# Top-k attention with two feed-forward networks on one core: low parts of late expert weights and relu outputs move from GpSimd to VectorE

## Chip, core and metric

The kernel runs on one core of a Trainium2 chip. The metric is the time of one execution on the device in microseconds (us), as the median of several runs. The engines are named as in the profile: PE is TensorE (PEld its weight loads), DVE is VectorE, ACT is ScalarE, POOL is GpSimd, SP is SyncE, which here only issues DMAs.

## What is computed

Attention with 8 heads over two sequences of 576 positions keeps, per row, only the 32 largest scores. Its output (1152 tokens of 512 values) goes through four gated experts and then through a network with three first matrices whose outputs are joined by a maximum. The matrices of that last network are handed over as 64-bit floats.

```python
scores = q @ k.T / sqrt(64); kth = 32nd largest of each row
attn = softmax(where(scores >= kth, scores, -1e9)); x = attn @ v        # -> (1152, 512)
p = probs / probs.sum(-1)
for e in range(4):                                                      # w1: 512 x 1024, w2: 1024 x 512
    out += p[:, e] * (relu(x @ w1[e]) @ w2[e])
h = maximum(maximum(out @ m1, out @ m2), out @ m3)                      # 512 x 768 each
result = h @ mo
```

## The kernel before

**Three products for one.** A matmul in float32 is replaced by three matmuls in a faster type (`product`, lines 677 to 683). Each operand is split in a high part, a copy in that type made by ScalarE, and a low part, the operand less its high part. TensorE then adds high x low, high x high and low x high (L681 to L683). So every weight and every activation needs a high part from ScalarE and a low part from VectorE or GpSimd before TensorE can go on.

**Tiles and stages.** The tokens are nine tiles of 128. The experts' work goes in stages of one to three tiles, as attention delivers them: stage 0 is tile 0, stages 1 to 6 are pairs of neighbours, stage 7 is tiles 6, 7 and 8, stage 8 is tiles 7 and 8. Each stage applies two of the four experts (`HALVES`), even stages units 0 to 3 and odd ones 4 to 7, a unit being half an expert, 512 hidden columns in two weights for the first layer (keys "a") and two for the second ("b"). Each key is a block of 128 x 1024 values. Attention is over when stage 7 begins. After stage 8 comes the last network in three groups of three tiles, with keys "c" for its first layer and "d" for its second. At its border the sums of the experts are turned on TensorE and split, the low part by L908.

**One weight.** `w_split_to` (257 to 282) walks through the list of keys in the order in which TensorE uses them, four keys ahead of the use (`weight`, `W_AHEAD`). For each it takes a raw buffer that SP's queue has loaded (`w_load_to`, L213; five raw buffers), lets ScalarE make the high part (L272) and then VectorE or GpSimd the low part (L278), into one of five buffers each. `LATE` is 7, and `late` (L274) counts keys from the first "a" key of stage 7. Before that key GpSimd makes all low parts, in two halves of 512 columns. From it on, odd keys go to VectorE in one instruction of 1024 columns and even keys to GpSimd. From stage 7 to the end of the experts there are 34 such keys, two "a" and two "b" by turns; then the "c" and "d" keys follow.

**One relu output.** `half1` makes the first layer of one key. Ordinarily ScalarE writes the relu of the PSUM result as high part (L823), and VectorE takes the relu of the PSUM result again and subtracts the high part (L825). Every fourth time (`ON_POOL_H`) ScalarE writes the relu in full to SBUF (L816), copies it as high part (L817), and GpSimd subtracts (L818). Three tiles need two PSUM banks and so two pieces in L823 and L825. `half2` and `layer2` are the second layer; `gated` (L742, L744) adds its output, times the gate, to the tile's sum.

**Conversions.** The last network's weights come as 64-bit floats. `to_float32` turns them into 32-bit ones in 48 pieces, most of them beside stages 7 and 8: two ScalarE steps (L239, L240), three VectorE steps (L242, L244, L246), one GpSimd step (L249), then a load for a later piece on SP's queue (L223) and a store to memory on ScalarE's queue (L254), each emitted some steps after the one before.

**What sets the order.** Each engine runs its instructions in the order in which the program emits them, and so does each DMA queue. The main loop (992 to 1015) emits a step of attention or conversions, then products until a planner's TensorE time (`pe`) has reached a goal that grows with its VectorE time (`dve`). After attention, each step adds a fixed pause of 0.8 and what was booked for conversions and evacuations. `later` delays the evacuation of a PSUM result by one or more products.

Of the kernel before, what the change touches and what calls it, by code (L numbers as in the profile page):

```python
# [24 lines left out]
ON_POOL_H = 4  # L25
# [5 lines left out]
LATE = 7  # L31
# [29 lines left out]
def kernel(  # L61
# [14 lines left out]
    nc = tc.nc  # L76
# [54 lines left out]
    def dve(n):  # L131
        clock["dve"] += 0.07 + n / 960.0

    def pe(n):
        clock["pe"] += n / 2400.0

    def bank(name):
        return pg.tile([P, 512], F32, tag="g", name=name)
# [62 lines left out]
    def whole(key):  # L201
        return key[1] in "ab" and key[0] in WHOLE

    def w_load_to(n):
        while w_pos["load"] < min(n, len(order)):
            key, src = order[w_pos["load"]]
            if key[1] in "cd" and narrowed[0] < WIDE * (narrow_at[key[2:]] + 1):
                return
            if whole(key):
                w_pos["load"] += 1  # L210
                continue
            raw = wp.tile([P, 1024], F32, tag="raw", bufs=5, name="raw")
            nc.sync.dma_start(out=raw, in_=src)  # L213
            w_raw[key] = raw
            w_pos["load"] += 1
# [41 lines left out]
    def w_split_to(n):  # L257
        while w_pos["split"] < min(n, len(order)):
            w_load_to(w_pos["split"] + 1)
            if w_pos["load"] == w_pos["split"]:  # L260
                return
            key, src = order[w_pos["split"]]
            if whole(key):
                w_hl[key] = wp.tile([P, 1024], F32, tag=("hi", "lo")[key[3]], name="whole")
                nc.sync.dma_start(out=w_hl[key], in_=src)
                w_pos["split"] += 1
                w_load_to(w_pos["split"] + 3)
                continue
            raw = w_raw.pop(key)
            hi = wp.tile([P, 1024], F32R, tag="hi", name="whi")  # L270
            lo = wp.tile([P, 1024], F32R, tag="lo", name="wlo")
            nc.scalar.activation(out=hi, in_=raw, func=AF.Copy)  # L272

            late = w_pos["split"] - w_index[LATE, "a", HALVES[LATE][0], 0]  # L274
            on = nc.vector if late >= 0 and late % 2 else nc.gpsimd

            for x in (slice(0, 512), slice(512, 1024)) if on is nc.gpsimd else (slice(0, 1024),):
                on.tensor_tensor(out=lo[:, x], in0=raw[:, x], in1=hi[:, x].bitcast(F32), op=ALU.subtract)  # L278
            f = 512 if key[1] in "bd" else 256
            w_hl[key] = (hi.rearrange("p (a f) -> p a f", f=f), lo.rearrange("p (a f) -> p a f", f=f))  # L280
            w_pos["split"] += 1
            w_load_to(w_pos["split"] + 3)

    def weight(key, oldest=None):

        w_split_to(w_index[oldest or key] + W_AHEAD + 2 * whole(key))
        return w_hl[key]
# [90 lines left out]
    def xs_of(tiles):  # L378

        at_ = [place(t) for t in tiles]  # L380
        step = max(1, at_[-1] - at_[0]) // max(1, len(at_) - 1)
        assert at_ == list(range(at_[0], at_[-1] + 1, step))
        return [[x[:, a].rearrange("p (s n) -> p s n", n=P)[:, at_[0]:at_[-1] + 1:step] for a in range(KT)] for x in xring]
# [279 lines left out]
    def tick():  # L663
        for x in list(lag):
            x.pop(0)()
            if not x:
                lag.remove(x)
# [5 lines left out]
    def later(*stages):  # L673
        tick()
        lag.append(list(stages))
# [20 lines left out]
    def layer1(wt, xs, N, ps=None):  # L696

        if ps is not None:
            for f in range(2):
                product(spread(ps[:, f * N:(f + 1) * N], xs[0][KT - 1]), [w[:, KT - 1, f * P:(f + 1) * P] for w in wt], [x[KT - 1] for x in xs], False, f == 1)  # L700
            yield [(slice(0, 2 * N), ps[:, 0:2 * N])]
            return
        groups = []
        for f in range(2):
            if not f or 2 * N > 512:
                ps = bank("ps1")
                groups.append((slice(f * N, 2 * N if 2 * N <= 512 else (f + 1) * N), ps[:, 0:min(2 * N, 512) if 2 * N <= 512 else N]))
            to = ps[:, f * N:(f + 1) * N] if 2 * N <= 512 else ps[:, 0:N]
            for a in range(KT):
                product(spread(to, xs[0][a]), [w[:, a, f * P:(f + 1) * P] for w in wt], [x[a] for x in xs], a == 0, a == KT - 1)  # L710
            yield groups if f else None

    def hidden(N):
        if 2 * N <= 512:
            ht = hp_.tile([P, 2, 512], F32R, tag="h", bufs=4, name="h")
            return ht[:, 0, 0:2 * N], ht[:, 1, 0:2 * N]

        assert len(x_ready) == len(pairs) and 2 * N <= 2 * WIDTH
        hh = kv.tile([P, 2, S], F32R, tag="kT", bufs=5, name="hh")
        hl = hp_.tile([P, 2, 512], F32R, tag="h", bufs=4, name="hl")  # L720
        return [x.rearrange("p a n -> p (a n)")[:, 0:2 * N] for x in (hh, hl)]
# [25 lines left out]
    def first_alone():  # L747
# [26 lines left out]
        for e, h in hs.items():  # L774
            ps = po.tile([P, DM], F32, tag="o", name="ps2")
            for y in range(2):
                for u in range(2):
                    w = w_alone["b", 2 * e + y, u]
                    for f in range(2):
                        pe(4 * DM)  # L780
                        nc.tensor.matmul(ps, lhsT=h[:, y, (2 * u + f) * P:(2 * u + f + 1) * P], rhs=w[f],
                                         start=y == u == f == 0, stop=y == u == f == 1)
                        yield True
                    if u:
                        w_split_to(2 * e + y + 1)
                    if e and not y and not u:
                        tick()
            later(gated(ps, 0, e, not e, False))

    def experts():  # L790
        begin = {}

        def half1(c, i, u):
            tiles = STAGES[c]
            N = len(tiles) * P
            if c in WHOLE:
                ps = bank("ps1")
                w = weight((c, "a", i, u)).rearrange("p (a f) -> p a f", f=256)
                for f in range(2):
                    for a in range(KT):  # L800
                        pe(4 * P)
                        nc.tensor.matmul(ps[:, f * P:(f + 1) * P], lhsT=w[:, a, f * P:(f + 1) * P], rhs=xfull[:, a, :], start=f == a == 0, stop=f == 1 and a == KT - 1)
                    yield True
                h = hp_.tile([P, 2, 512], F32, tag="h", bufs=4, name="hfull")[:, 0, 0:2 * P]
                later(lambda: [nc.scalar.activation(out=h, in_=ps[:, 0:2 * P], func=AF.Relu), made.add(("h", c, i, u))])
                yield h
                return
            for groups in layer1(weight((c, "a", i, u)), xs_of(tiles), N, begin.pop((c, i, u), None)):
                if groups is None:
                    tick()  # L810
                    yield True
            hh, hl = hidden(N)
            count = made_h[0] = made_h[0] + 1
            if ON_POOL_H and not count % ON_POOL_H:
                raw = ms.tile([P, 2 * WIDTH], F32, tag="tm", bufs=2, name="raw")
                later(lambda: [nc.scalar.activation(out=raw[:, g], in_=ps, func=AF.Relu) for g, ps in groups],  # L816
                      lambda: [nc.scalar.activation(out=hh[:, 0:2 * N], in_=raw[:, 0:2 * N], func=AF.Copy),  # L817
                               nc.gpsimd.tensor_tensor(out=hl[:, 0:2 * N], in0=raw[:, 0:2 * N], in1=hh[:, 0:2 * N].bitcast(F32), op=ALU.subtract),  # L818
                               made.add(("h", c, i, u))])
                yield hh, hl  # L820
                return
            dve(2 * N)
            later(lambda: [nc.scalar.activation(out=hh[:, g], in_=ps, func=AF.Relu) for g, ps in groups],  # L823
                  *[lambda: None] * H_LAG,
                  lambda: [nc.vector.scalar_tensor_tensor(out=hl[:, g], in0=ps, scalar=0.0, in1=hh[:, g].bitcast(F32),  # L825
                                                          op0=ALU.max, op1=ALU.subtract) for g, ps in groups]
                  + [made.add(("h", c, i, u))])
            yield hh, hl
# [252 lines left out]
```

## Time and profile before

| | before |
|---|---|
| median of three runs | 765.25 us (765.12 to 765.64) |
| the profiled execution | 765.73 us |
| its span (first to last instruction) | 763.9 us |
| busy: PE, PEld | 729.3, 644.0 us |
| busy: DVE, ACT, POOL | 625.9, 508.2, 503.3 us |
| read from memory, written | 120.60, 8.65 MB |

The span is what the profile covers; 1.8 us of the execution lie around it. Stage 7's first matmul starts at 475.5 us of the span and the last network's first one at 606.3 us. A busy engine may also be an engine that waits inside an instruction. Matmuls are pipelined, so the distance between the starts of two matmuls, and not the duration of one, tells TensorE's pace.

### The profile page before, as it was taken

How to read it: one execution, taken by the hardware profiler on the slowest of the kernel's cores; microseconds unless marked ns; L12 is line 12 of the kernel's file. 1: busy time of each engine (PE TensorE's matmuls, PEld its weight loads, DVE VectorE, ACT ScalarE, POOL GpSimd, SP SyncE). 2: the span in 40 equal slices, each digit the busy share in tenths (PEclk: the TensorE clock that was granted, in tenths of full speed). 3: DMA queues.
4: the chain of work that ended last, by engine and by line, in shares of the span. 5: the costliest groups of instructions: out<-in, count | busy, mean ns of one | idle time of the engine just before them, and what ended most of it. 6: DMA issues, size and time to landing. Idle time of an engine off the chain costs nothing. (4 is left out here: it accounts for less than half of the span.)

```text
span 763.9 us, 13775 instructions
## 1 busy us (share of the span) xinstructions
PE 729.3 (95%) x4758; PEld 644.0 (84%) x4758; DVE 625.9 (82%) x1161; ACT 508.2 (67%) x1137; POOL 503.3 (66%) x433
## 2 busy tenths in 40 slices
PE   6899999999999999999999979999999899999998
PEld 3576789888989999888899868998797699999996
DVE  6999989989999899999999979999999844233341
ACT  4668889899896888787788674765656533433431
POOL 2514788599979778788688759867869742442520
PEclk9999999999999999999999999999999999999999
DMA  7693564545637364464445457887878652453501
GB/s 219 183 275 133 160 193 136 149 152 174 183 110 214 97 189 126 135 190 124 146 122 163 137 187 218 274 266 239 291 229 290 209 168 85 134 183 97 193 2 42
DMA packets 56486, 130.16 MB, mean 170 GB/s; under 512 B 9760, under 2 KB 23328, under 8 KB 56416
## 3 DMA queue, kind: packets, MB, share of 16 engines
q1 hardware_dynamic: 48064, 120.69, 50.8%
q10 hardware_dynamic: 8352, 8.59, 3.2%
q8 instruction: 37, 0.61, 0.3%
q14 instruction: 33, 0.27, 0.1%
HBM read 120.60 MB, written 8.65 MB: 169 GB/s over the span
## 5 line engine op out<-in xcount | busy, mean ns | idle before, releaser
L278 POOL TENSOR_TENSOR wlo<-raw,whi 128x512 fp32r<-128x512 f32 x258 | 341.1, 1351 | 116.6 <-ACT whi L272 112.5
L272 ACT ACTIVATE whi<-raw 128x1024 fp32r<-128x1024 f32 x164 | 169.5, 1056 | 47.2 <-POOL narrow L249 19.1
L681 PE MATMUL ps<-xl,whi 128*128 128x256 f32 (+1 forms) x584 | 173.5, 297 | 0.4 <-POOL xl L556 0.4
L682 PE MATMUL ps<-xh,whi 128*128 128x256 f32 (+1 forms) x584 | 170.7, 292 | 0.0
L683 PE MATMUL ps<-xh,wlo 128*128 128x256 f32 (+1 forms) x584 | 170.7, 292 | 0.0
L444 DVE MAX8 m<-work 128x8 f32<-128x576 f32 x216 | 155.0, 743 | 0.1
L681 PEld LDWEIGHTS ps<-xl,whi 128*128 128x128 f32 x584 | 110.7, 190 | 1.5 <-POOL xl L556 0.6
L682 PEld LDWEIGHTS ps<-xh,whi 128*128 128x128 f32 x584 | 109.7, 188 | 0.8 <-issue 0.2
L683 PEld LDWEIGHTS ps<-xh,wlo 128*128 128x128 f32 x584 | 109.6, 188 | 0.0
L446 DVE MATCH_REPLACE8 work<-m,work 128x576 f32<-128x576 f32 x144 | 106.5, 740 | 0.0
L278 DVE TENSOR_TENSOR wlo<-raw,whi 128x1024 fp32r<-128x1024 f32 x35 | 55.5, 1586 | 50.5 <-ACT whi L272 38.2
L681 PE MATMUL ps<-wlo,h 128*128 128x512 f32 x224 | 92.9, 415 | 4.0 <-POOL wlo L278 2.2
L683 PE MATMUL ps<-whi,h 128*128 128x512 f32 x224 | 89.7, 400 | 5.4 <-POOL h L818 5.4
L682 PE MATMUL ps<-whi,h 128*128 128x512 f32 x224 | 89.2, 398 | 0.0
L249 POOL TENSOR_TENSOR narrow<-narrow,raw 128x256 int32<-128x256 int32 x48 | 50.4, 1050 | 32.8 <-DVE narrow L246 10.7
L431 ACT ACTIVATE s<-pss 128x288 f32<-128x288 f32 x144 | 51.4, 400 | 11.4 <-PE pss L419 11.1
L444 DVE MAX8 m<-s 128x8 f32<-128x576 f32 x72 | 53.8, 747 | 4.9 <-ACT s L431 4.9
L683 PEld LDWEIGHTS ps<-whi,h 128*128 128x128 f32 x224 | 42.9, 192 | 17.1 <-POOL h L818 7.5
L681 PEld LDWEIGHTS ps<-wlo,h 128*128 128x128 f32 x224 | 43.6, 195 | 14.9 <-POOL wlo L278 5.6
L446 DVE MATCH_REPLACE8 work<-m,s 128x576 f32<-128x576 f32 x72 | 53.3, 740 | 0.0
L681 PE MATMUL ps<-x2l,whi 128*128 128x384 f32 x144 | 48.8, 339 | 1.3 <-DVE x2l L908 1.3
L948 DVE TENSOR_TENSOR tm<-ps,tm 128x384 f32<-128x384 f32 x36 | 19.9, 555 | 35.2 <-PE ps L683 33.3
(113 smaller groups left out, 1551.9 us busy)
## 6 DMA issues: line engine op xcount, KB each, us to landing
raw<-in_w_dram SPq DMA_DIRECT2D x128, 512.0 KB, 4.1
raw<-narrow SPq DMA_DIRECT2D x36, 512.0 KB, 4.1
raw<-in_m_dram SPq DMA_DIRECT2D x36, 256.0 KB, 4.0
whole<-in_w_dram SPq DMA_DIRECT2D x14, 512.0 KB, 5.7
narrow<-narrow ACTq DMA_DIRECT2D x48, 128.0 KB, 4.1
kraw<-in_k_dram SPq DMA_DIRECT2D x16, 288.0 KB, 4.5
qraw<-in_q_dram SPq DMA_DIRECT2D x48, 64.0 KB, 3.8
raw<-in_mo_dram SPq DMA_DIRECT2D x12, 256.0 KB, 4.7
```

The costliest lines, as they stand in the source:

```text
L249: nc.gpsimd.tensor_tensor(out=out.bitcast(I32), in0=out.bitcast(I32), in1=last, op=ALU.add)
L272: nc.scalar.activation(out=hi, in_=raw, func=AF.Copy)
L278: on.tensor_tensor(out=lo[:, x], in0=raw[:, x], in1=hi[:, x].bitcast(F32), op=ALU.subtract)
L431: nc.scalar.activation(out=s[:, h, :], in_=halves[h][:, 0:SH], func=AF.Copy)
L444: nc.vector.max(m[:, 8 * r:8 * r + 8], src)
L446: nc.vector.match_replace(out=self.w[j], in_to_replace=m[:, 8 * r:8 * r + 8], in_values=src, imm_value=NEG)
L681: nc.tensor.matmul(ps, lhsT=lh, rhs=rl, start=first, stop=False)
L682: nc.tensor.matmul(ps, lhsT=lh, rhs=rh, start=False, stop=False)
L683: nc.tensor.matmul(ps, lhsT=ll, rhs=rh, start=False, stop=last)
L948: nc.vector.tensor_tensor(out=tm[:, g], in0=ps, in1=tm[:, g], op=ALU.max)
```

## The change

The low parts of the "a" and "b" keys from the first one of stage 7 on all go to VectorE. The "c" and "d" keys still alternate. From stage 7 on every relu output is made the ordinary way (L823, L825).

```diff
             late = w_pos["split"] - w_index[LATE, "a", HALVES[LATE][0], 0]
-            on = nc.vector if late >= 0 and late % 2 else nc.gpsimd
+            on = nc.vector if late >= 0 and (late % 2 or key[1] in "ab") else nc.gpsimd
...
             count = made_h[0] = made_h[0] + 1
-            if ON_POOL_H and not count % ON_POOL_H:
+            if ON_POOL_H and not count % ON_POOL_H and c < LATE:
                 raw = ms.tile([P, 2 * WIDTH], F32, tag="tm", bufs=2, name="raw")
```

## Rows read from the trace of the kernel before

**Rows 1.** Windows: busy us (x count) of PE, PEld, DVE, ACT, POOL; clock; DMA

```profile
596.00:599.50 3.50, 1.18 (x5) 0.33 (x3) 3.36 (x6) 2.96 (x9) 2.13 (x3) 1.00 0.80 253
599.50:603.30 3.80, 3.80 (x10) 3.00 (x11) 2.69 (x5) 3.39 (x6) 3.52 (x3) 0.55 0.01 4
...
474.00:605.00 131.00, 124.39 (x668) 108.26 (x666) 127.22 (x164) 79.73 (x153) 102.19 (x81) 0.99 0.79 256
606.30:764.00 157.70, 153.95 (x834) 146.16 (x834) 55.40 (x71) 54.95 (x77) 55.14 (x38) 1.00 0.35 118
```

**Rows 2.** TensorE's waits in 474 to 606.5 us: us in total, times, longest

```profile
PE ps L683 <- POOL hl L818: 2.3, 2, 1.8
PE ps L683 <- POOL h L818: 2.1, 2, 1.2
PE ps L681 <- ACT h L817: 1.4, 1, 1.4
PE ps L681 <- DVE x2l L908: 1.3, 1, 1.3
PE ps L681 <- POOL wlo L278: 0.5, 1, 0.5
PE ps L681 <- DVE wlo L278: 0.2, 1, 0.2
```

**Rows 3.** Line 818, 474 to 605 us: ns min/median/max, first and last start

```profile
L818 POOL TENSOR_TENSOR h<-raw,h x3: 1323/1461/1476, 484.2 to 598.1; 128x512 fp32r<-128x512 f32 x3
```

**Rows 4.** Single lines, 474 to 605 us: ns min/median/max, first and last start

```profile
L246 DVE SCALAR_TENSOR_TENSOR narrow<-raw,narrow x40: 424/426/1487, 473.0 to 604.7; 128x256 uint32<-128x256 uint32 x40
...
L278 DVE TENSOR_TENSOR wlo<-raw,whi x18: 1211/1424/2322, 474.4 to 601.5; 128x1024 fp32r<-128x1024 f32 x18
...
L825 DVE SCALAR_TENSOR_TENSOR hl<-ps,hh x12: 540/543/550, 488.8 to 536.1; 128x384 fp32r<-128x384 f32 x12
L825 DVE SCALAR_TENSOR_TENSOR h<-ps,h x6: 677/680/685, 551.7 to 592.4; 128x512 fp32r<-128x512 f32 x6
...
L244 DVE TENSOR_SCALAR narrow<-raw x39: 293/727/1821, 477.6 to 604.4; 128x256 uint32<-128x256 uint32 x39
...
L242 DVE SCALAR_TENSOR_TENSOR raw<-narrow,raw x39: 408/593/1509, 476.6 to 602.8; 128x256 f32<-128x256 f32 x39
...
L249 POOL TENSOR_TENSOR narrow<-narrow,raw x40: 735/814/1736, 475.5 to 599.8; 128x256 int32<-128x256 int32 x40
```

**Rows 5.** Timeline of TensorE: start us, us, engine, line [idle before and releaser]

```profile
470.33 0.40 PE L681 MATMUL ps<-wlo,h 128*128 128x512 f32 x1
470.57 0.39 PE L682 MATMUL ps<-whi,h 128*128 128x512 f32 x1
...
550.24 0.50 PE L683 MATMUL ps<-whi,hl 128*128 128x512 f32 x1 [1.76 <-POOL hl L818]
```

**Rows 6.** Timeline of GpSimd and VectorE side by side, 466 to 471 us

```profile
466.47 5.47 POOL L278 TENSOR_TENSOR wlo<-raw,whi 128x512 fp32r<-128x512 f32 x4
...
469.39 1.40 DVE L246 SCALAR_TENSOR_TENSOR narrow<-raw,narrow 128x256 uint32<-128x256 uint32 x1
```

**Rows 7.** GpSimd's groups, 474 to 605 us: busy us, mean ns, idle before

```profile
L278 POOL TENSOR_TENSOR wlo<-raw,whi 128x512 fp32r<-128x512 f32 x36 | 52.4, 1478 | 1.0 <-ACT whi L272 0.6
...
L818 POOL TENSOR_TENSOR h<-raw,h 128x512 fp32r<-128x512 f32 x3 | 4.3, 1420 | 0.0
L818 POOL TENSOR_TENSOR hl<-raw,hh 128x768 fp32r<-128x768 f32 x2 | 4.0, 2013 | 0.0
```

**Rows 8.** VectorE's groups, 474 to 605 us: busy us, mean ns, idle before

```profile
L246 DVE SCALAR_TENSOR_TENSOR narrow<-raw,narrow 128x256 uint32<-128x256 uint32 x40 | 31.9, 797 | 1.4
L278 DVE TENSOR_TENSOR wlo<-raw,whi 128x1024 fp32r<-128x1024 f32 x18 | 29.7, 1651 | 1.1 <-POOL narrow L249 1.1
L244 DVE TENSOR_SCALAR narrow<-raw 128x256 uint32<-128x256 uint32 x39 | 28.3, 725 | 1.3
L242 DVE SCALAR_TENSOR_TENSOR raw<-narrow,raw 128x256 f32<-128x256 f32 x39 | 27.7, 709 | 0.0
```

## The prediction

> **What bounds the kernel now.** I read the stretches of the span first, then TensorE's waits, then VectorE's and GpSimd's groups and the durations of single lines. The changed lines act from about 472 us (the first weight of stage 7) to about 605 us (the last weight of the experts). In 474 to 605 us VectorE is busy 127.2 of 131 us and GpSimd 102.2; TensorE is busy too, 124.4, but that is the engine with the work that can't be moved [rows 1]. After 606 us TensorE is busy 154.0 of 157.7 us and VectorE a third of the time [rows 1], so time won before 606 us is kept.
>
> What TensorE loses in the stretch is the second thing to see. It waits 2.3 and 2.1 us for the low parts of relu outputs that GpSimd makes (L818), 1.4 us for ScalarE's copy in front of one of them (L817), 0.5 and 0.2 us for low parts of weights, and 1.3 us for the low part of the turned x2 at the border to the last network [rows 2]. GpSimd makes five such relu parts in this stretch [rows 7], the first of them, at 484 us, still for stage 6 [rows 3]. VectorE makes 12 by L825 (six of stage 7 in two pieces, six of stage 8 in one) [rows 4], and none has a line among TensorE's waits [rows 2].
>
> The third is the clock. In 596.0 to 599.5 us TensorE was busy only 1.18 us, because of two of those waits; in the next 3.8 us its granted clock was 0.55, mostly the 1.2 GHz level, and it issued 10 matmuls [rows 1]. At the full clock such 512-column matmuls start 0.23 us apart [rows 5].
>
> The fourth is why VectorE is full. Its operations with both inputs in SBUF take 0.42 us (L246) or 1.21 us (L278) at the least, but up to 1.49 and 2.32 us [rows 4]. The long ones lie beside GpSimd: four L278 halves run from 466.47 for 5.47 us, and an L246 that begins at 469.39 takes 1.40 us [rows 6]. Operations that read PSUM (L825) keep one duration, 0.54 and 0.68 us, to 10 ns [rows 4]. So GpSimd and VectorE wait for one another, one instruction at a time.
>
> **The change part by part.** Weight keys come in fours (a, a, b, b), 34 of them from the first of stage 7 on; odd ones are on VectorE already, so 17 move.
>
> GpSimd loses 34 halves at 1.478 us, 50.3 us, and four relu parts, 2 x 1.42 + 2 x 2.01 = 6.9 us [rows 7]. It goes from 102.2 to about 45 us in this stretch. By itself that ends nothing; it counts by what waited behind it.
>
> VectorE gains 17 x 1.211 = 20.6 us of weight parts, and for the relu parts 4 x 0.543 + 2 x 0.680 = 3.5 us (two of stage 7 in two pieces, two of stage 8 in one): 24.1 us [rows 4].
>
> VectorE loses its waits for GpSimd. L246, L278, L244 and L242 took 31.9 + 29.7 + 28.3 + 27.7 = 117.6 us [rows 8]. At their least durations they would take 40 x 0.424 + 18 x 1.211 + 39 x 0.293 + 39 x 0.408 = 66.1 us [rows 4]. The excess is 51.5 us. What stays is the last step of the conversion on GpSimd (L249), 40 times. The trace has no stretch with L249 alone beside the new mix, so I bound it: nothing if it falls beside PSUM reads, and its whole least duration each time, 40 x 0.735 = 29.4 us [rows 4]. I take 0.43 us each, the median of L244 less its least, since that median comes from pairs with L249: 17.2 us. VectorE would then be busy 127.2 - 51.5 + 24.1 + 17.2 = 117.0 us, between 99.8 and 129.2. Now it takes 127, so the added work fits only because the waits go. The Trainium skill (SBUF — State Buffer, section Who interferes with whom) has the meeting of the two engines as a lock on a shared port that is held for a whole instruction while the other blocks. The trace agrees as far as rows 6 go; taken at its hardest, with every L249 starting just ahead of a VectorE operation, the rule gives the upper end, 129.2, and my 117.0 takes the shorter waits that the median of L244 shows.
>
> TensorE's side gives the sum. The waits on L818 go, 4.4 us, and the 1.4 us on L817, because the relu part is then made like the other 12: one ScalarE step and one VectorE step instead of two and a GpSimd step. After each of those five waits the first matmul takes 0.50 us instead of 0.39 [rows 5], so 0.5 us more. Without the waits at 596 to 599.5 us I expect no clock drop behind them: 3.8 - 10 x 0.23 = 1.5 us. The 0.7 us on low parts of weights I leave as they are: a late VectorE takes GpSimd's place. The 1.3 us at the border stays as well; the low part of x2 stands in VectorE's queue behind conversions and weight parts that do not move.
>
> New waits: each moved weight part waits on VectorE for ScalarE's high part, and behind it in that queue stand conversions, the relu parts and the sums into the accumulators, which TensorE and ScalarE need. In this stretch VectorE idles so far only 1.1 us, before one L278, and that for GpSimd [rows 8]. The bounds are nothing, and all that is won; I take 1.0 us, nearest to what the 18 weight parts already there cost.
>
> Edits at nothing: four ScalarE copies go (ScalarE is busy 79.7 of 131 us [rows 1]). One instruction of 1024 columns takes 1.21 us where two halves took 2.96, so no low part comes later for that. A raw weight buffer is now freed by VectorE; SP's queue, where the next loads stand, already waits mostly for GpSimd's L249, which comes sooner. L254's store on ScalarE's queue waits for the same step. The planner counts 2.9 us more VectorE time (four sets of 0.87 or 0.60), so some one conversion is issued later against the products: about 1.1 us of VectorE work moves behind 605 us, where VectorE is idle for most of the time. Without that cover it would cost the 1.1 us.
>
> The sum: 4.4 + 1.4 + 0.5 + 1.5 - 1.0 = 6.8 us. The profiled execution took 765.73 us (span 763.9 and 1.8 around it), 0.48 above the median of 765.25. So 758.9 for a like execution, and **758.5 us** as a median.
>
> **The rivals.**
> *All waits go.* Weight parts and the border too, nothing new: 4.4 + 1.4 + 0.5 + 1.5 + 0.7 + 1.3 = 9.8, 755.4 us. For it: VectorE at 117 us is below what TensorE needs, about 123. Against: the border hangs on a queue that hardly changes.
>
> *Half comes back.* A weight part waits at the head of VectorE's queue for its high part and holds a relu part: half of the 6.8 is lost, 761.9 us. For it: ScalarE itself is held by stores that wait for conversions. Against: VectorE has not waited for ScalarE in this stretch [rows 8].
>
> *Same.* VectorE's relu parts come as late as GpSimd's did, because VectorE runs behind: 765 us. Against: none of the 12 was waited for.
>
> *Slower.* VectorE becomes the bound in stages 7 and 8. It decides from the point where its waits for L249 exceed 27.4 us (99.8 of work without them, 3.8 idle as now, 131 of stretch). If all forty block for a whole L249, 29.4 us, the stretch is 133.0 us and the time 767.3 us. For it: VectorE is at 97% and gets more work. Against: the 51.5 us of waits lie mostly beside the GpSimd halves that go. The Trainium skill (Perfetto Trace Analysis, section Optimizing Scalar/DVE Operations) advises the opposite of this change, to offload a saturated VectorE, though it adds that between these two engines it might not help, for the shared port. By the first half alone, with none of the waits gone, the 24.1 us would be added: 789.4 us. No row bears that out so far.
>
> That the change does something else than it says has little room: the keys before stage 7 and those of the last network keep their engine, and I have counted them so.
>
> **How the numbers follow.** Forecast, 756.5 to 760.5 us: 0.57. All waits go: 0.12. Half comes back: 0.13. Same: 0.07. Slower: 0.11. About 0.2%, 1.5 us, is what a measurement can tell here. Faster by more is the first three, 0.82; within it 0.07; slower 0.11. The range of 755.0 to 764.0 leaves out the slower case, most of the same case and a sliver below: some 0.2.
>
> **What would show it.** In 474 to 605 us of the changed kernel: of L818 only the one for stage 6; GpSimd busy about 45 us; about 35 weight parts on VectorE with durations mostly near 1.21 us; VectorE busy less than before or as much; L246 mostly near 0.42; no granted clock near 0.55 before the border; the first product of the last network some 7 us earlier, with the same distance from there to the end. It is wrong if VectorE is busy throughout with its short operations as long as now, if TensorE waits for L825 or for VectorE's weight parts by microseconds, or if the gain is lost after 606 us.

## The result and the profile after

The changed kernel takes 755.8 us (755.3 to 758.7), the kernel before beside it 765.4. The ratio to the kernel before is 0.9876, with a 95% interval of 0.9845 to 0.9907: faster by about 9.6 us, where 6.8 were forecast. That is inside the range of 755.0 to 764.0, but below the 756.5 to 760.5 that the forecast itself was given. The profiled execution of the changed kernel took 758.65 us (span 756.7), its slowest of four, 7.1 us below the profiled one of before. Its granted clock over the span was 0.992, against 0.998 in the other three, which took 755.3 to 756.1 us.

The stretches of the changed kernel, in the columns of [rows 1], with the border now at 597.3 us:

```profile
474.00:541.00 67.00, 67.00 (x341) 60.65 (x340) 63.54 (x106) 42.59 (x83) 29.91 (x26) 1.00 0.86 284
541.00:590.00 49.00, 49.00 (x314) 44.29 (x313) 46.27 (x77) 30.00 (x58) 16.35 (x14) 1.00 0.85 289
590.00:597.50 7.50, 5.10 (x24) 3.86 (x22) 5.75 (x9) 6.62 (x11) 6.54 (x5) 1.00 0.30 93
597.50:601.30 3.80, 3.80 (x14) 3.80 (x15) 3.61 (x7) 0.11 (x1) 1.27 (x2) 0.58 0.93 302
474.00:597.30 123.30, 121.06 (x673) 108.76 (x671) 115.36 (x189) 79.21 (x150) 52.60 (x45) 1.00 0.82 274
597.30:756.70 159.40, 155.62 (x834) 147.82 (x834) 55.95 (x75) 53.98 (x76) 54.22 (x39) 0.98 0.35 117
```

TensorE has no idle time from 474 to 590 us, at the full clock. GpSimd fell to 52.6 us in the stretch. VectorE, with 25 more instructions than in [rows 1], fell from 127.2 of 131.0 us to 115.4 of 123.3.

TensorE's waits in 474 to 606 us of the changed kernel, against the six lines of [rows 2]:

```profile
PE ps L681 <- DVE x2l L908: 2.4, 1, 2.4
```

Five lines are gone, and the border is 1.1 us worse. Why VectorE has room is in its groups in 474 to 597 us, which answer to [rows 8]:

```profile
L278 DVE TENSOR_TENSOR wlo<-raw,whi 128x1024 fp32r<-128x1024 f32 x34 | 43.4, 1292 | 4.0 <-ACT whi L272 3.9
L242 DVE SCALAR_TENSOR_TENSOR raw<-narrow,raw 128x256 f32<-128x256 f32 x39 | 22.3, 571 | 0.0
L246 DVE SCALAR_TENSOR_TENSOR narrow<-raw,narrow 128x256 uint32<-128x256 uint32 x39 | 17.5, 450 | 1.3
L244 DVE TENSOR_SCALAR narrow<-raw 128x256 uint32<-128x256 uint32 x39 | 17.3, 444 | 1.3
```

L246 fell from 0.797 us in the mean to 0.450, L278 from 1.651 to 1.292. Sixteen more weight parts cost 13.7 us net of what the others became shorter.

The length of the two stages is best read from two starts, stage 7's first matmul and the last network's first. Timeline of TensorE, kernel before:

```profile
475.53 0.34 PE L681 MATMUL ps<-xl,whi 128*128 128x384 f32 x1
...
606.29 0.45 PE L681 MATMUL ps<-x2l,whi 128*128 128x384 f32 x1 [1.31 <-DVE x2l L908]
```

And the changed kernel:

```profile
476.70 0.34 PE L681 MATMUL ps<-xl,whi 128*128 128x384 f32 x1
...
597.46 0.45 PE L681 MATMUL ps<-x2l,whi 128*128 128x384 f32 x1 [2.40 <-DVE x2l L908]
```

That is 130.8 us before and 120.8 after: 10.0 us won in the two stages. This execution gave some back outside: it reached stage 7 1.2 us later, and behind the border the granted clock was 0.58 for 14 matmuls in 3.8 us, which at the usual 0.17 us apart would be 2.4. A second profile of the changed kernel (span 753.4 us) has the same 120.8 us; it reached stage 7 at 475.1 us and took 157.5 us from the border to the end, where the first took 159.2 and the kernel before 157.6.

### The profile page after: what moved, and what is told of

The parts are those of the page before. It is cut to its first block, busy times and chain, and to the rows that moved or that the text cites. A ratio compares the mean times of both kernels' runs of the same rounds, so it can differ in the third digit from the quotient of the medians.

```text
span 756.7 us, 13765 instructions
## 1 busy us (share of the span) xinstructions
PE 727.7 (96%) x4758; PEld 646.1 (85%) x4758; DVE 614.5 (81%) x1184; ACT 505.6 (67%) x1133; POOL 450.5 (60%) x395
## 4 chain that ended last, share of the span: by engine, by line
PE 49%; DVE 24%; ACT 13%; issue 6%; POOL 6%; DMA 2%; ACTq 0%; POOLq 0%; DVEq 0%
PE ps L681 12%; PE ps L683 12%; PE ps L682 12%; DVE m L444 11%; DVE work L446 8%; POOL wlo L278 4%; ACT whi L272 4%; PE pso L682 2%; PE pso L681 2%; PE psa L766 2%; PE pso L683 2%; PE pss L419 1%; ACT pt L493 1%; DMA raw<-in_w_dram 1%; DVE h L825 1%
## 5 line engine op out<-in xcount | busy, mean ns | idle before, releaser
L278 POOL TENSOR_TENSOR wlo<-raw,whi 128x512 fp32r<-128x512 f32 x224 | 291.2, 1330 | 121.2 <-ACT whi L272 119.9
L278 DVE TENSOR_TENSOR wlo<-raw,whi 128x1024 fp32r<-128x1024 f32 x52 | 70.9, 1372 | 55.4 <-ACT whi L272 39.3
L249 POOL TENSOR_TENSOR narrow<-narrow,raw 128x256 int32<-128x256 int32 x48 | 52.5, 1095 | 74.1 <-DVE narrow L246 26.7
L681 PEld LDWEIGHTS ps<-wlo,h 128*128 128x128 f32 x224 | 43.6, 195 | 10.6 <-POOL wlo L278 4.0
L682 PE MATMUL ps<-x2h,whi 128*128 128x384 f32 x144 | 49.3, 342 | 0.0
```

The lines of the kernel that those rows point to most:

```text
L249: nc.gpsimd.tensor_tensor(out=out.bitcast(I32), in0=out.bitcast(I32), in1=last, op=ALU.add)
L681: nc.tensor.matmul(ps, lhsT=lh, rhs=rl, start=first, stop=False)
L682: nc.tensor.matmul(ps, lhsT=lh, rhs=rh, start=False, stop=False)
```

## The experiments

Two theories stood against each other at first. Theory A: what costs is that VectorE and GpSimd take turns, and the weight halves fill GpSimd. Theory B, the sum of the prediction: the waits belong to the relu part's longer way over GpSimd.

**Each edit alone.** The first edit without the second:

```diff
-            if ON_POOL_H and not count % ON_POOL_H and c < LATE:
+            if ON_POOL_H and not count % ON_POOL_H:
```

> Only the first edit: 17 more weight parts on VectorE, the five relu parts stay on GpSimd. Theory A (the root is that VectorE and GpSimd take turns, and the weight halves are what fills GpSimd): L246 mostly near 0.43 us, VectorE's excess over least durations falls from 51.5 us to under 20, the waits on L818 fall from 4.4 us to under 2, and the time comes within 2 us of the changed kernel, 755.5 to 758. Theory B (the sum of the prediction: the waits belong to the longer chain of a relu part on GpSimd): the 5.8 us on L818 and L817 stay and the time is 763 to 766.

Measured: 759.2 us, ratio 0.9900 (0.9872 to 0.9929). And the second without the first:

```diff
-            on = nc.vector if late >= 0 and (late % 2 or key[1] in "ab") else nc.gpsimd
+            on = nc.vector if late >= 0 and late % 2 else nc.gpsimd
```

> Only the second edit: no relu parts on GpSimd from stage 7 on, the weight parts alternate as before. Theory B: nearly all of the gain, waits on L818 and L817 gone with their clock drop, 757.5 to 759.5. Theory A: VectorE stays busy over 95% of the stretch with L246 near 0.8 us in the mean; the waits move to L825 or to weight parts; 761 to 765.5.

Measured: 762.9 us, ratio 0.9959 (0.9940 to 0.9978). TensorE's waits with the relu edit alone, 474 to 615 us:

```profile
PE ps L681 <- DVE hl L825: 2.7, 1, 2.7
PE ps L681 <- DVE x2l L908: 2.4, 1, 2.4
PE ps L683 <- DVE h L825: 0.7, 1, 0.7
```

and VectorE's L246 there:

```profile
L246 DVE SCALAR_TENSOR_TENSOR narrow<-raw,narrow 128x256 uint32<-128x256 uint32 x38 | 28.1, 738 | 1.3
```

The relu parts moved, VectorE stayed nearly as held up as before, and TensorE now waits for L825 where it had waited for L818. The longer wait, at 516 us, is before a matmul that does not read the part (`ps<-xl,whi`); it seems to need the PSUM bank that L825 still has to read. The two stages:

```profile
476.45 0.34 PE L681 MATMUL ps<-xl,whi 128*128 128x384 f32 x1
...
602.55 0.44 PE L681 MATMUL ps<-x2l,whi 128*128 128x384 f32 x1 [2.36 <-DVE x2l L908]
```

126.1 us, 4.7 fewer than before and not 10.0. Theory B, which wanted nearly all of the gain from this edit, fails here. The time of the first edit alone lay between its two expectations, with three of its four executions above 758.5, so it was run again beside the changed kernel.

> The changed kernel once more, beside the first edit alone on one chip. If the weight halves carry the gain and the relu edit adds nothing (theory A in its strict form), the two differ by less than 1 us. If the relu edit has a gain of its own (theory B in part), this one is 2 to 4 us faster than the first edit alone. 755.5 to 757.

> The first edit alone, again. Strict theory A: 755.5 to 757, as the changed kernel beside it. Theory B in part: 758 to 760, with waits on L818 or L817 between 474 and 597 us in the slower executions.

Measured: 755.4 us, ratio 0.9867 (0.9844 to 0.9891), and 757.4 us, ratio 0.9876 (0.9854 to 0.9897). The medians are 2 us apart, more than strict theory A allowed, but the ratios' intervals overlap almost wholly. The stretch itself decides. Timeline of TensorE, first edit alone:

```profile
475.44 0.34 PE L681 MATMUL ps<-xl,whi 128*128 128x384 f32 x1
...
596.13 0.54 PE L681 MATMUL ps<-x2l,whi 128*128 128x384 f32 x1 [2.33 <-DVE x2l L908]
```

120.7 us, as with both edits. Its relu parts on GpSimd, in 474 to 597 us:

```profile
L818 POOL TENSOR_TENSOR h<-raw,h x3: 1337/2279/2293, 481.3 to 587.6; 128x512 fp32r<-128x512 f32 x3
L818 POOL TENSOR_TENSOR hl<-raw,hh x2: 2067/2072/2076, 511.2 to 541.9; 128x768 fp32r<-128x768 f32 x2
```

The three of 512 columns are slower than in [rows 3] (2.28 us at the median against 1.46), the two of 768 took 2.07 against 2.01 in [rows 7], and TensorE waits for none of them. So before, they came late because the two engines ran behind, not because the way was long. In the two stages the second edit adds nothing on top. The 2 us between the medians lie behind the border: both traces of the first edit alone took 159.4 to 159.5 us from there to the end, with a granted clock of 0.66 and 0.72 in 597 to 602 us; the two of the changed kernel took 159.2 us (0.66) and 157.5 (1.00). Whether the second edit makes that drop of the clock rarer is not shown.

**GpSimd's work put back without its results.** The changed kernel, and for each moved weight two subtractions that nobody needs:

```diff
+            if late >= 0 and not late % 2 and key[1] in "ab":
+                for _ in range(2):
+                    nc.gpsimd.tensor_tensor(out=x, in0=x, in1=x, op=ALU.subtract)
```

(`x` stands for the 512 columns of `xfull`, which is no longer used then.)

> The changed kernel, and for each moved weight GpSimd runs two subtractions of 512 columns from SBUF to SBUF that nobody waits for (34 in all, some 1.4 us each), on a tile that is no longer used. Theory A: VectorE waits for them as it did for the weight halves, its two-input operations are long again (L246 mean over 0.7 us), its load passes the stretch of 131 us (127 plus up to 24), and the time is 766 to 785. A rival by which GpSimd matters only through what it produces: as the changed kernel, 755 to 758.

Measured: 774.0 us, ratio 1.0101 (1.0080 to 1.0122). That is 18 us more than the changed kernel, with no one waiting for GpSimd's new work. GpSimd's and VectorE's groups, 474 to 597 us (numbers of later lines are four higher):

```profile
L278 DVE TENSOR_TENSOR wlo<-raw,whi 128x1024 fp32r<-128x1024 f32 x31 | 44.9, 1468 | 0.1
...
L244 DVE TENSOR_SCALAR narrow<-raw 128x256 uint32<-128x256 uint32 x34 | 21.5, 634 | 1.2
L246 DVE SCALAR_TENSOR_TENSOR narrow<-raw,narrow 128x256 uint32<-128x256 uint32 x34 | 20.4, 601 | 1.2
...
L281 POOL TENSOR_TENSOR xfull<-xfull 128x512 f32<-128x512 f32 x34 | 44.5, 1309 | 1.4
```

and TensorE's longest waits, 474 to 615 us:

```profile
PE ps L685 <- DVE hl L829: 4.9, 1, 4.9
PE ps L685 <- DVE wlo L278: 4.6, 4, 1.5
```

L246 at 0.60 us fell short of the 0.7 expected, but the time and the new waits for VectorE are theory A's, and so is VectorE's load: it was busy 136.2 of the 139.0 us from 474 to 613, where the last network now began. This is the slower rival of the prediction, made real: VectorE's added load without the relief.

**The same with fills.** In place of the two subtractions, five `nc.gpsimd.memset` of the same tile.

> The changed kernel, and for each moved weight GpSimd runs five fills of 512 columns that read nothing (some 2.7 us together, estimated from a 128x256 fill of 0.32 us), so it is about as busy as in the run beside it. Theory A, with waits only between two reads of SBUF: VectorE's durations stay least, 755 to 759. If GpSimd's mere business, or its writes, hold VectorE up: as the run with subtractions, 766 to 785.

Measured: 759.1 us, ratio 0.9912 (0.9891 to 0.9932). Groups in 474 to 597 us:

```profile
L244 DVE TENSOR_SCALAR narrow<-raw 128x256 uint32<-128x256 uint32 x39 | 20.9, 536 | 1.3
L246 DVE SCALAR_TENSOR_TENSOR narrow<-raw,narrow 128x256 uint32<-128x256 uint32 x39 | 18.0, 461 | 1.3
...
L281 POOL MEMSET xfull<- 128x512 f32 x85 | 45.4, 534 | 4.0
```

GpSimd is as busy as beside it (45.4 us of added work against 44.5), and the time is 15 us better. So it is the reading that holds VectorE up, for the operations with two inputs: L246 is at 0.461 us, 0.011 above the changed kernel's, where the subtractions added 0.151. L244, with one input, went from 0.444 to 0.536. The fills are also shorter than the subtractions (0.53 us against 1.31), but that does not explain L246: fills ran in 45.4 of these 123 us, so an operation that had to wait for them would lose, by an estimate from these figures, 0.37 times half of 0.534, about 0.10 us. L244 lost about that, L246 did not.

The Trainium skill (SBUF — State Buffer, section Who interferes with whom) says that an operation with two SBUF inputs contends with a GpSimd instruction that reads and not with one that only writes, which L246 bears out. The same section of the Trainium skill says that operations in a two-port mode contend with GpSimd, which would cover L244. Its least duration, 0.293 us against 0.424 of L246 on as many elements, would fit such a mode, but no run here shows it. Some 3 us were lost against the changed kernel in the medians; 1.7 of them are in the two stages (122.4 us against 120.8), where TensorE waited 1.4 us for L829, the L825 of before. The rest lies outside and is not explained.

**The border.** One line after the sums are turned; `flush` emits at once what `later` has delayed:

```diff
         yield from turned_ahead(len(STAGES))
+        flush()
         for ti in range(len(STAGES[before[0]])):
```

> The changed kernel with one flush after the turned sums at the border to the last network, so that all high and low parts of x2 stand in ScalarE's and VectorE's queues ahead of the next weights and conversions. If the 2.4 us at the border are queueing behind those (my account), the wait falls under 0.5 us and the clock drop behind it goes too: 752 to 754.5. If it is the chain of transposes, ScalarE and VectorE by itself, the wait stays and the time with it, 755.5 to 757.

Measured: 752.8 us, ratio 0.9826 (0.9804 to 0.9848). VectorE's timeline there, changed kernel without the flush (the second run of it):

```profile
587.87 0.76 DVE L908 TENSOR_TENSOR x2l<-pst,x2h 128x384 fp32r<-128x384 f32 x2 [1.25 <-ACT x2h L907]
590.31 1.48 DVE L278 TENSOR_TENSOR wlo<-raw,whi 128x1024 fp32r<-128x1024 f32 x1 [1.69 <-ACT whi L272]
591.72 0.74 DVE L908 TENSOR_TENSOR x2l<-pst,x2h 128x384 fp32r<-128x384 f32 x2
592.38 0.85 DVE L242 SCALAR_TENSOR_TENSOR raw<-narrow,raw 128x256 f32<-128x256 f32 x1
593.27 0.71 DVE L244 TENSOR_SCALAR narrow<-raw 128x256 uint32<-128x256 uint32 x1
594.01 1.37 DVE L246 SCALAR_TENSOR_TENSOR narrow<-raw,narrow 128x256 uint32<-128x256 uint32 x1
595.31 0.74 DVE L908 TENSOR_TENSOR x2l<-pst,x2h 128x384 fp32r<-128x384 f32 x2
```

and with it (L908 is line 909):

```profile
587.91 2.08 DVE L909 TENSOR_TENSOR x2l<-pst,x2h 128x384 fp32r<-128x384 f32 x6 [1.25 <-ACT x2h L908]
590.89 1.48 DVE L278 TENSOR_TENSOR wlo<-raw,whi 128x1024 fp32r<-128x1024 f32 x1 [0.91 <-ACT whi L272]
```

The six low parts were done at 596.0 us with a weight and a conversion between them; in one row they are done at 590.0, before TensorE needs them at 593.4. The two stages took 118.2 us, 2.6 fewer than without the flush. Nothing of the arithmetic changed.

The flush on the kernel before:

> The kernel before with the flush alone. Its border wait was 1.3 us: 763.5 to 765 if that goes and nothing else changes. If the flush is worth the 3 us that it was worth on the changed kernel, 762 to 763.5: then the border wait was not made larger by the change but was hidden under another.

Measured: 763.6 us, ratio 0.9955 (0.9936 to 0.9974). The border wait is gone there too, and the L818 waits stay (4.0 and 2.3 us from 390 us on). The gain of some 2.8 us is more than the 1.3 us of that wait. The trace shows where the rest is: TensorE was busy 1.29 us in 596.0 to 599.5 us, about as little as in [rows 1], but in the next 3.8 us the granted clock was 1.00 and not 0.55. Whether the flush had a part in that is not shown; executions went from 762.1 to 766.6 us.

**Stage 6.** The bound of the second edit one stage lower, first without and then with the flush:

```diff
-            if ON_POOL_H and not count % ON_POOL_H and c < LATE:
+            if ON_POOL_H and not count % ON_POOL_H and c < 6:
```

> The changed kernel with the relu parts of stage 6 off GpSimd too (the bound in the second edit is one stage lower). The wait of 1.97 us on L818 at 457 us goes, and the drop of the clock behind it at times: 752 to 754.5. Rival: VectorE, which in stage 6 still has attention's sorting and one of two engines' turns with GpSimd, makes the part as late, so the wait moves to L825: 755 to 757.5.

Measured: 759.6 us, ratio 0.9921 (0.9892 to 0.9950), a miss. The wait at 457 us was gone, but the only wait from 474 us on had doubled:

```profile
PE ps L681 <- DVE x2l L908: 5.0, 1, 5.0
```

> Changed kernel, flush at the border, and no relu parts on GpSimd in stage 6 either. If the miss of the run with stage 6 alone came only from the border (5.0 us of waiting there instead of 2.4), the flush removes it and the 2 us of stage 6 show: 750 to 752.5. If the order of stage 6 costs by itself (its weights come late on GpSimd), 753 to 757.

Measured: 751.2 us, ratio 0.9788 (0.9762 to 0.9815), the fastest version of all. So the miss lay at the border and right behind it, where the granted clock of the run without the flush was 0.50 for 3.8 us. The first and last low parts of x2 on VectorE, kernel before and then the run without the flush:

```profile
599.62 0.74 DVE L908 TENSOR_TENSOR x2l<-pst,x2h 128x384 fp32r<-128x384 f32 x2
...
605.02 1.41 DVE L908 TENSOR_TENSOR x2l<-pst,x2h 128x384 fp32r<-128x384 f32 x4
```

```profile
586.88 0.76 DVE L908 TENSOR_TENSOR x2l<-pst,x2h 128x384 fp32r<-128x384 f32 x2 [1.56 <-ACT x2h L907]
...
596.77 0.74 DVE L908 TENSOR_TENSOR x2l<-pst,x2h 128x384 fp32r<-128x384 f32 x2
```

The six took 6.8 us before, 8.2 in the changed kernel and 10.6 here, where two conversions stand between them instead of one. TensorE came for them 5.4, 5.6 and 5.6 us after the first had begun, so the wait grew with what was emitted between them, not because TensorE came earlier.

**The first edit where VectorE is full of sorting.** Weight parts on VectorE from stage 6 on, with the flush:

```diff
-            on = nc.vector if late >= 0 and (late % 2 or key[1] in "ab") else nc.gpsimd
+            on = nc.vector if late >= 0 and late % 2 or w_pos["split"] >= w_index[6, "a", HALVES[6][0], 0] and key[1] in "ab" else nc.gpsimd
```

> Changed kernel with the flush, and the weight parts on VectorE from the first key of stage 6, 16 more. VectorE is also full in stage 6, but there with attention's sorting, whose durations are the same beside GpSimd (0.74 to 0.75 us). If only waits for GpSimd make room for weight parts, VectorE has no room there and the time rises over the run with the flush by 3 to 15 us: 756 to 768. If moving weight parts off GpSimd pays wherever GpSimd is full, 750 to 752.

Measured: 761.3 us, ratio 0.9915 (0.9888 to 0.9942), 8.5 us slower by the medians than the changed kernel with the flush. TensorE's longest wait, 390 to 610 us:

```profile
PE psv L532 <- ACT pt L498: 9.4, 3, 6.1
```

These are attention's transposed weights, and the sorting that comes ahead of them now shares VectorE with 14 weight parts (18.3 us in 400 to 474 us). GpSimd's busy time there fell from 57.2 to 17.3 us and bought too little: up to the start of stage 7 VectorE's three conversion steps, nine of each, fell from 22.4 to 12.4 us, against 23.1 us of weight parts. Stage 7 began at 484.5 us instead of 475.2, and from there to the border both kernels took 118.2.

## Why the prediction was right, and where its terms were off

**Direction, range and the mechanism on VectorE held.** VectorE did not become the bound, because its waits for GpSimd were worth more than its new work. The forecast for its load was 117.0 us and the trace shows 115.4. What stays of the excess over least durations is 43.4 - 34 x 1.215 + 22.3 - 39 x 0.409 + 17.5 - 39 x 0.424 + 17.3 - 39 x 0.293 = 15.3 us; 17.2 were taken for L249. GpSimd was forecast at 45 and came to 52.6: two pairs of the last network's weight halves now fall into the stretch instead of one (some 3 us), and L249 took 1.156 us in the mean against 1.096 (2.4 us in all). VectorE's four lines (least, median, most) in the changed kernel:

```profile
L278 DVE TENSOR_TENSOR wlo<-raw,whi x34: 1215/1219/1777, 476.1 to 591.9; 128x1024 fp32r<-128x1024 f32 x34
...
L246 DVE SCALAR_TENSOR_TENSOR narrow<-raw,narrow x39: 424/426/1372, 475.6 to 595.6; 128x256 uint32<-128x256 uint32 x39
...
L244 DVE TENSOR_SCALAR narrow<-raw x39: 293/295/759, 474.8 to 594.8; 128x256 uint32<-128x256 uint32 x39
L242 DVE SCALAR_TENSOR_TENSOR raw<-narrow,raw x39: 409/419/1514, 474.4 to 593.9; 128x256 f32<-128x256 f32 x39
```

The medians are the least durations now; in [rows 4] those of L244, L242 and L278 were 0.727, 0.593 and 1.424 us.

**The step that failed** is the one that gave the gain to the relu edit: "the relu part is then made like the other 12: one ScalarE step and one VectorE step instead of two and a GpSimd step". The last step ahead of a wait is what the profile names, and it was read as the cause. With the relu edit alone TensorE waited 3.4 us for L825, and the two stages became 4.7 us shorter; with the weight edit alone it waited for no L818, and they became 10.1 us shorter. The two edits were made together, so the total came near although the sum put it to the wrong one: that part of the hit is luck. The evidence offered, that none of the 12 L825 was waited for, said nothing of the other four places: the two L825 that TensorE waited for with the relu edit alone, at 516 and 596 us, are moved ones.

**The sizes.** The two stages became 10.0 us shorter, where the sum has 6.8. Three of its terms were too careful: the 0.7 us on low parts of weights went as well; new waits cost nothing rather than 1.0 (VectorE did wait 3.9 us for ScalarE's high parts, with TensorE still fed); and a wait costs more than its idle time. In the kernel before, the matmuls around the longest one are

```profile
548.08 0.40 PE L682 MATMUL ps<-whi,hh 128*128 128x512 f32 x1
550.24 0.50 PE L683 MATMUL ps<-whi,hl 128*128 128x512 f32 x1 [1.76 <-POOL hl L818]
```

2.16 us apart instead of 0.23: 1.93 us lost, 0.17 more than listed, because the idle time is counted from the end of the 0.40 us. The sum has only the 0.11 that the next matmul takes longer. Read from start to start in this way, the five relu waits cost 7.2 us where the sum has 6.3, and the waits for weights 1.4. One term went the other way. The border, expected to stay at 1.3 us, grew to 2.4: the conversions and weight parts that "do not move" did move, and VectorE's six low parts took 8.2 us there instead of 6.8. With these four the 6.8 become some 9 of the 10.0; the rest is spread over shorter gaps. The 1.5 us of the clock drop came out (some 1.6 by the starts), but that the waits must bring it is not shown: the kernel before with the flush had the same waits at the full clock.

**The rivals.** "All waits go" at 755.4 us has the right time, but not its reason: the border wait did not go. "Half comes back" and "same" did not come. "Slower" did not come with this change, though the run with GpSimd's reads put back shows that its condition is real: 774.0 us, beyond the 767.3 of its price, since more than L249 stood in the way. The Trainium skill (Perfetto Trace Analysis, section Optimizing Scalar/DVE Operations) says that offloading work from a saturated VectorE may make sense, but might not help between VectorE and GpSimd, which share a port. Stages 7 and 8 go against the first half, as VectorE's busy time there was to a good part waiting; stage 6, where most of it was sorting, agrees with it: there the added weight parts cost 8.5 us.

## What to carry to other kernels

A busy share of 97% does not say that an engine has 3% left: compare the durations of one form with its least, and what lies above may be waiting that goes when the neighbour's work goes. Two engines that read SBUF by turns are best counted as one, and work is put on the one that does it in less time (1.2 us on VectorE against 2.6 to 3.0 in two halves on GpSimd), unless the other engine's work is of a kind that does not wait. The instruction that a wait names is the last step and not always the cause, so each edit is worth a run alone; and when a stretch becomes faster, look at the next border, where other work emitted between the parts that it needs can take a part of the gain.

## What was not expected of the hardware

Useless subtractions on GpSimd, 44.5 us of them with nobody waiting for a result, cost some 18 us of the whole kernel's time; as many microseconds of fills cost about 3, of which 1.7 are seen in the two stages. A GpSimd instruction can be the one that suffers, too: with the first edit alone L818 took 2.28 us at the median against 1.46 before. And a drop of the granted clock followed the border wait of 2.4 us in one profile of the changed kernel (0.58 for 3.8 us) and not in the second, which had the same wait (1.00 for the 3.8 us behind it); executions of one kernel differ by some 3 us here, and that is a part of it.
